# A decode layer over 2,048 cached positions: a K load moved forward, a reordering of the attention output, and a new split of the last weight rows over the DMA engines

## The chip, the cores and the metric

The kernel runs on one core of a Trainium2 chip. The metric is the time of one execution in device microseconds (us). Times of different kernels are compared only when they were taken on the same chip in alternating rounds, and the kernel before runs again beside each of them. Some executions fall into a slower group. Fast executions are compared with fast ones.

The words used throughout: TensorE multiplies matrices and leaves the result in a small memory, PSUM; VectorE and ScalarE (DVE and ACT in the profile) work element by element. A load brings data into the on-chip memory SBUF in pieces, one per DMA engine, and *lands* when the last piece has arrived. The granted clock is the share of its full clock that TensorE was given, 0.5 or 1.0 in these traces.

## The reference, cut to what matters

A layer normalization feeds two branches that are added to the input: attention over the last 2,048 cached positions, and an MLP with a squared ReLU.

```python
# B=2, Sq=1, D=576, Hq=32, Hkv=16, Sk=8192, Dh=128, F=4608; everything bfloat16
W = min(4096, max(256, Sk // 4))                     # 2048
q = (xn @ wq)                                        # 576 x 4096
k, v = the last W positions of each head's cache, each shared by two query heads
o = softmax(q k^T * Dh**-0.5) v
A = o @ wo                                           # 4096 x 576
B = relu(xn @ w1 + b1)**2 @ w2 + b2                  # w1: 576 x 4608, w2: 4608 x 576
return x + A + B
```

There are only two rows of activations, so nearly all the work is to read 53.6 MB of caches and weights once.

## The kernel before

The caches are cut into eight K units and eight V units of 2 MB (four heads of one batch row each). Everything big is issued on one queue in a fixed order, and each load is split over the sixteen DMA engines. TensorE transposes a K unit, multiplies it by the queries (`sc_ps`), and two steps later multiplies the probabilities by V (`o_ps`). The parts that the change touches:

```python
# o of one unit: o_ps is 128 x 512, four blocks of 128; row r is valid in one of the four blocks
def pv_sum(u):                      # sums of exp over the key chunks, and their reciprocal
    sc_ps = sc_tiles.pop(u)
    matmul(sc_ps[:, 0:1], lhsT=same_c[:], rhs=l_tiles.pop(u)[:], start=True, stop=True, ...)
    nc.vector.reciprocal(out=linv[:], in_=sc_ps[:, 0:1])

def pv_end(u):
    nc.vector.tensor_scalar(out=o_sb (128 x 512), in0=o_ps[:], scalar1=linv, op0=ALU.mult)
    def fin():
        for k in range(NS):         # NS = 4 fp32 products with the weights o_sb: o as 128 x 8
            matmul(o_ps[:, 0:NC], lhsT=o_sb[:, k, :], rhs=sel_o[:, k, :], start=(k == 0), stop=(k == NS - 1), ...)
        nc.vector.tensor_copy(out=oG_tiles[tq][:, :, b], in_=o_ps[:, 0:NC])

def wo_sel(t):                      # bring o onto wo's partitions: 16 selection products per half
    rr = oG * rmask                 # two VectorE operations
    for h in range(2 * NC):
        matmul(wps[:], lhsT=sel[:, MZ - h * DW:MZ - h * DW + P], rhs=rr[:, :, h * B:(h + 1) * B], ...)
    nc.vector.tensor_copy(out=ws[:, :, 0:MB:BS], in_=wps[:])
# ... cut ...
XR, XP, XE = 8, 32, 8               # the last 256 rows of w2: 4 small loads of 8 pieces of 9,216 B
w2x_sb = const.tile([XP, XR * D], BF16, name="w2x_sb")
# ... cut ...
    for u in range(2, NU - 1):
        step(u)                     # transposes, scores and softmax of unit u; o of unit u - 2
        if u + 1 < NU - 1:
            load_v(u + 1)
        if u == 4:
            issue_wo(0)
            for i in range(NW):
                issue_w1(i)
        if u + 3 < NU:
            load_k(u + 3)           # the last K unit is queued behind wo and w1
        if u == 5:
            load_v(NU - 1)
    issue_wo(1)
    for w in W2P:                   # w2: three blocks of 9 x 128 rows, then 4, 2 and 1 x 128 rows
        issue_w2(*w)
    mlp_h_start(); pv_all(NU - 3); wo_sel(0); wo_acc(0)
    # ... h = relu(w1 x + b1)^2 ...
    step(NU - 1, with_pv=False)     # the last K unit, late
    pv_all(NU - 2); mlp_x(); pv_all(NU - 1)
    wo_sel(1); wo_acc(1)
    for w in W2P[:NG4 - 1]:
        mlp_o(*w)                   # three big w2 blocks into out_ps
    # four copies of out_ps into part, then mlp_tail: the last 7 x 128 rows, then one addition
```

`mlp_x` multiplies the 256 rows of `w2x_sb`. In the profile the four part copies are `part<-out_ps`, the last rows are `tail_ps<-w,hT_sb` and the addition is `fin_sb<-tail_ps,part`.

## Time and profile before

| | kernel before |
|---|---|
| timed executions | 134.98, 135.18, 137.09 us |
| the profiled execution | 136.98 us, span 135.19 us, marked slow |
| moved by DMA | 53.76 MB in 4,419 packets |
| TensorE, VectorE, ScalarE busy | 99.4, 56.6, 46.5 us |
| last load landed | 129.72 us |

The span runs from the first to the last instruction in the profile. It is about 1.8 us shorter than the time of the same execution (136.98 less 135.19). A row of the groups gives engine, line and operation, then output and inputs with shapes and count, then the busy sum in us and the mean of one in ns, and at last the idle time just before and who ended it. These two groups of the kernel before bring o of a unit from one layout into another, eight times 1.1 and 0.75 us:

```profile
L104 PE MATMUL o_ps<-sel_o,o_sb 128*128 128x8 f32 x64 | 9.1, 268 | 2.9 <-DVE o_sb L398 2.9
...
L398 DVE TENSOR_SCALAR o_sb<-o_ps,linv 128x512 f32<-128x512 f32 x8 | 6.0, 750 | 2.2 <-PE o_ps L104 1.7
```

### The profile page before, as it was taken

To read this page: it belongs to the slowest core of one execution; us is meant where nothing else is said; L and a number is where in the kernel's file an instruction comes from. 1 tells how busy PE (TensorE), PEld (TensorE's weight loads), DVE (VectorE), ACT (ScalarE), POOL (GpSimd) and SP (SyncE) were. 2 spreads that over 40 slices of the span, in tenths; PEclk is the share of its full clock that TensorE was granted. 3 is DMA by queue.
4 is the path that set the end of the run, shared out by engine and by line. 5 is a ranking of instruction groups with operands and counts; after the bars stand their busy time and mean duration, and the time that the engine had idled before them with its cause. 6 is when DMAs were issued, how large, how long until landed. Compare 5 with 4: busy or idle time off the path is not lost.

```text
span 135.2 us, 2258 instructions
## 1 busy us (share of the span) xinstructions
PE 99.4 (74%) x939; PEld 64.6 (48%) x939; DVE 56.6 (42%) x154; ACT 46.5 (34%) x65; POOL 5.5 (4%) x18
## 2 busy tenths in 40 slices
PE   0067747979759779877897897788529976977980
PEld 0065423455427455545554574554229744454660
DVE  7934405254482565484393574510052446022010
ACT  6714502178275085093372462200032522000000
POOL 7000000010100100100100100100000001000000
PEclk9999975579999999999999999856985599555599
DMA  4999999999999999999999999999999999999800
GB/s 151 393 419 439 441 415 441 417 441 427 431 427 439 422 427 436 417 446 419 431 431 431 436 426 431 425 431 411 441 427 427 436 439 426 408 433 430 325 13 1
DMA packets 4419, 53.76 MB, mean 398 GB/s; under 512 B 531, under 2 KB 662, under 8 KB 1178
## 3 DMA queue, kind: packets, MB, share of 16 engines
q1 hardware_dynamic: 4320, 53.32, 92.9%
q10 hardware_dynamic: 90, 0.31, 0.6%
q8 instruction: 7, 0.11, 0.3%
q14 instruction: 2, 0.02, 0.0%
HBM read 53.62 MB, written 0.00 MB: 397 GB/s over the span
## 4 chain that ended last, share of the span: by engine, by line
DMA 40%; PE 36%; DVE 14%; issue 3%; SPq 2%; ACT 2%; POOL 1%; POOLq 0%; ACTq 0%; DVEq 0%
DMA w_rem<-in_B_w_dram 27%; DMA wq<-in_A_wq_dram 12%; PE kT_ps L107 12%; PE out_ps L104 7%; PE sc_ps L104 7%; PE o_ps L104 6%; DVE kT L338 4%; DVE o_sb L398 2%; PE q_ps L104 2%; DVE m L357 2%; DVE pT L371 1%; SPq L132 1%; DVE qrow L302 1%; SPq L125 1%; DVE hrow L463 1%
## 5 line engine op out<-in xcount | busy, mean ns | idle before, releaser
L107 PE MATMUL kT_ps<-ident_f,k 128*128 128x128 f32 x256 | 41.4, 310 | 7.7 <-DVE kT L338 3.4
L107 PEld LDWEIGHTS kT_ps<-ident_f,k 128*128 128x128 f32 x256 | 32.6, 160 | 20.6 <-DVE kT L338 5.7
L336 ACT COPY kT<-kT_ps 128x1024 bf16<-128x1024 bf16 x32 | 31.5, 1013 | 20.6 <-PE kT_ps L107 20.6
L338 DVE COPY kT<-kT_ps 128x1024 bf16<-128x1024 bf16 x32 | 21.5, 681 | 15.3 <-PE kT_ps L107 15.3
L104 PE MATMUL sc_ps<-kT,qz 128*32 128x512 bf16 x128 | 10.6, 415 | 5.8 <-DVE kT L338 5.6
L368 ACT ACTIVATE p<-sc_ps,bias 128x512 bf16<-128x512 f32 x8 | 5.5, 687 | 23.1 <-DVE gown L364 19.5
L104 PE MATMUL o_ps<-sel_o,o_sb 128*128 128x8 f32 x64 | 9.1, 268 | 2.9 <-DVE o_sb L398 2.9
L104 PEld LDWEIGHTS o_ps<-sel_o,o_sb 128*128 128x128 f32 x64 | 8.8, 214 | 4.8 <-DVE o_sb L398 4.8
L104 PE MATMUL o_ps<-v,pT 128*32 128x512 bf16 x128 | 10.2, 414 | 0.0
L357 DVE TENSOR_REDUCE m<-sc_ps 128x1 f32<-128x512 f32 x8 | 5.5, 691 | 7.6 <-PE sc_ps L104 7.6
L104 PE MATMUL out_ps<-wo,ws 128*17 128x288 bf16 x64 | 8.0, 442 | 0.7 <-DVE ws L432 0.7
L371 DVE STREAM_TRANSPOSE pT<-p 128x512 bf16<-128x512 bf16 x8 | 5.7, 710 | 5.1 <-ACT p L368 5.1
L104 PEld LDWEIGHTS <-qz 128*32 128x32 bf16 x128 | 2.6, 98 | 9.9 <-DVE kT L338 7.2
L361 POOL PARTITION_ALL_REDUCE gmax<-m x8 | 2.9, 366 | 106.4 <-DVE m L359 106.4
L398 DVE TENSOR_SCALAR o_sb<-o_ps,linv 128x512 f32<-128x512 f32 x8 | 6.0, 750 | 2.2 <-PE o_ps L104 1.7
L601 ACT COPY part<-out_ps 17x144 f32<-17x144 f32 x2 | 0.5, 268 | 18.1 <-DVE part L601 18.1
L104 PEld LDWEIGHTS <-xnT 128*2 128x2 bf16 x100 | 3.0, 92 | 7.8 <-issue 6.7
L104 PEld LDWEIGHTS <-ws 128*17 128x17 bf16 x64 | 4.4, 133 | 3.5 <-issue 0.5
L407 DVE CAST oG<-o_ps 128x8 bf16<-128x8 f32 x8 | 1.4, 170 | 10.2 <-PE o_ps L104 10.2
L463 DVE TENSOR_TENSOR hrow<-t 98x384 bf16<-98x384 f32 x3 | 1.6, 556 | 9.6 <-ACT t L462 9.5
L107 PE MATMUL pro_ps<-ident,tmp_x 2*128 2x2 bf16 x6 | 0.5, 174 | 6.6 <-DVE tmp_x L230 6.6
L462 ACT ACTIVATE t<-h_ps 98x384 f32<-98x384 f32 x3 | 1.4, 488 | 11.5 <-PE h_ps L104 11.2
(88 smaller groups left out, 73.6 us busy)
## 6 DMA issues: line engine op xcount, KB each, us to landing
k<-in_A_k_cache_dram SPq DMA_DIRECT2D x8, 2048.0 KB, 16.3
v<-in_A_v_cache_dram SPq DMA_DIRECT2D x8, 2048.0 KB
wo<-in_A_wo_dram SPq DMA_DIRECT2D x2, 2304.0 KB
w<-in_B_w_dram SPq DMA_DIRECT2D x2, 2304.0 KB, 36.0
wq<-in_A_wq_dram SPq DMA_DIRECT2D x2, 2048.0 KB
w<-in_B_w_dram SPq DMA_DIRECT2D x3, 1296.0 KB, 31.3
w_rem<-in_B_w_dram SPq DMA_DIRECT2D x1, 576.0 KB
w<-in_B_w_dram SPq DMA_DIRECT2D x1, 576.0 KB
```

Source lines behind the costliest of these rows:

```text
L104: tc.keep_in_program_order(nc.tensor.matmul(*a, **k))
L107: tc.keep_in_program_order(nc.tensor.transpose(*a, **k))
L336: nc.scalar.copy(out=kT, in_=kT_ps[:])
L338: nc.vector.tensor_copy(out=kT, in_=kT_ps[:])
L357: nc.vector.tensor_reduce(out=m1[:], in_=sc_ps[:], axis=AX.X, op=ALU.max)
L361: nc.gpsimd.partition_all_reduce(gmax[:], m2[:], channels=P, reduce_op=ReduceOp.max)
L368: nc.scalar.activation(out=p_sb[:], in_=sc_ps[:], func=ACT.Exp, bias=bias[:, 0:1], scale=scale, accum_out=l1[:])
L371: nc.vector.transpose(out=pT[:].rearrange("p j r -> p (j r)"), in_=p_sb[:])
L398: nc.vector.tensor_scalar(out=o_sb[:].rearrange("p s d -> p (s d)"), in0=o_ps[:], scalar1=o_tiles.pop((u, 0))[:, 0:1], scalar2=None, op0=A ...
L407: nc.vector.tensor_copy(out=oG_tiles[tq][:, :, b], in_=o_ps[:, 0:NC])
L462: nc.scalar.activation(out=t1, in_=mlp["ps"][k][0:RB, :], func=ACT.Relu)
L463: nc.vector.tensor_tensor(out=hrow[:, k * HB:(k + 1) * HB], in0=t1, in1=t1, op=ALU.mult)
```

## The change

Three things are changed. **The order:** the last K unit is loaded and worked on ahead of wo and w1, so that at the end of the stream only V units and weights are left. **The product:** VectorE adds the four blocks of `o_ps` into one 128 x 128 tile under a mask. One fp32 product of 129 columns, of which the 129th is the row of sums, brings that onto the partitions that wo wants, and the division comes last. The row sums no longer need the scores' PSUM bank. **The split:** of the last 256 rows of w2, 96 go as four loads of eight pieces (3,456 B each) and 160 as four loads of five (9,216 B each). Before, all went as four loads of eight pieces of 9,216 B. The intent there is to leave less on three of the eight engines concerned.

```diff
-    XR, XP, XE = 8, 32, 8
-    FT = (HW - XR * XP) // P
+    XS = ((3, 32, 8), (8, 20, 5))
+    FT = (HW - sum(r * p for r, p, _ in XS)) // P
 ... (cut: the rows' bookkeeping, tiles renamed, PSUM banks dealt out anew, b2 put on x's tile)
-    w2x_sb = const.tile([XP, XR * D], BF16, name="w2x_sb")
-    const.tile([P, 120], F32, name="pad_1")
+    w2x_sb = [const.tile([xp, xr * D], BF16, name=f"w2x_sb_{i}") for i, (xr, xp, _) in enumerate(XS)]
+    const.tile([P, 24], F32, name="pad_1")
 ... (cut)
-        o_sb = work.tile([P, NS, Dh], F32, tag="o_sb", name=f"o_sb_{u}")
-        nc.vector.tensor_scalar(out=o_sb[:].rearrange("p s d -> p (s d)"), in0=o_ps[:],
-                                scalar1=o_tiles.pop((u, 0))[:, 0:1], scalar2=None, op0=ALU.mult)
+        o1 = o1_tiles.pop(u)
+        for k in range(NS):
+            kw = dict(out=o1[:, 0:Dh], in0=o_ps[:, k * Dh:(k + 1) * Dh])
+            if k == 0:
+                nc.vector.tensor_scalar(scalar1=in_s[:, 0:1], scalar2=None, op0=ALU.mult, **kw)
+            else:
+                nc.vector.scalar_tensor_tensor(scalar=in_s[:, k:k + 1], in1=o1[:, 0:Dh], op0=ALU.mult, op1=ALU.add,
+                                               **kw)
 
         def fin():
-            for k in range(NS):
-                matmul(o_ps[:, 0:NC], lhsT=o_sb[:, k, :], rhs=sel_o[:, k, :], start=(k == 0), stop=(k == NS - 1),
-                       skip_group_check=True)
 ... (cut)
+            matmul(op_tiles[t][:, b, :], lhsT=of_h[:, z:z + P], rhs=o1[:], start=(i == 0 and b == 0), stop=(i == 1),
+                   skip_group_check=True)
 ... (cut: pv_sum and the selection products of wo_sel go; reciprocal, mask, product and sum on VectorE come)
-    for u in range(2, NU - 1):
+    for u in range(2, NU):
         step(u)
-        if u + 1 < NU - 1:
+        if u + 1 < NU - 2:
             load_v(u + 1)
+        if u + 3 < NU:
+            load_k(u + 3)
         if u == 4:
             issue_wo(0)
             for i in range(NW):
                 issue_w1(i)
-        if u + 3 < NU:
-            load_k(u + 3)
         if u == 5:
-            load_v(NU - 1)
+            for v in (NU - 2, NU - 1):
+                load_v(v)
+    wo_sel(0)
+    wo_acc(0)
     issue_wo(1)
 ... (cut)
-    step(NU - 1, with_pv=False)
     pv_all(NU - 2)
     mlp_x()
```

## The prediction

> **What bounds the kernel now.** I read the page first: the engines, then the slices, then the chain of work that ended last.
>
> ```profile
> PE 99.4 (74%) x939; PEld 64.6 (48%) x939; DVE 56.6 (42%) x154; ACT 46.5 (34%) x65; POOL 5.5 (4%) x18
> ...
> PEclk9999975579999999999999999856985599555599
> DMA  4999999999999999999999999999999999999800
> GB/s 151 393 419 439 441 415 441 417 441 427 431 427 439 422 427 436 417 446 419 431 431 431 436 426 431 425 431 411 441 427 427 436 439 426 408 433 430 325 13 1
> ...
> DMA 40%; PE 36%; DVE 14%; issue 3%; SPq 2%; ACT 2%; POOL 1%; POOLq 0%; ACTq 0%; DVEq 0%
> ```
>
> No compute engine is full. The row of the sixteen DMA engines is full from the second slice to the 37th, at 410 to 446 GB/s. The kernel moves 53.76 MB, and at 430 GB/s that alone is 125 us. So the kernel is bound by its stream of loads, plus whatever comes after the stream. The question is how long the program goes on after the last byte. For that I took the busy time by stretch (PE busy, PEld, DVE, ACT, POOL, PEclk, DMA share, GB/s) and the timeline of the last 20 us:
>
> ```profile
> 115.00:120.00 5.00, 4.14 (x34) 1.84 (x28) 0.92 (x2) 0.00 (x0) 0.00 (x0) 0.50 0.99 420
> ...
> 125.00:126.00 1.00, 1.00 (x12) 0.59 (x10) 0.00 (x0) 0.00 (x0) 0.00 (x0) 0.50 0.95 395
> 126.00:127.00 1.00, 1.00 (x12) 0.58 (x8) 0.00 (x0) 0.00 (x0) 0.00 (x0) 0.50 0.90 365
> 127.00:128.00 1.00, 1.00 (x12) 0.59 (x10) 0.00 (x0) 0.00 (x0) 0.00 (x0) 0.51 0.80 304
> 128.00:129.00 1.00, 1.00 (x20) 0.77 (x18) 0.00 (x0) 0.00 (x0) 0.00 (x0) 1.00 0.29 92
> 129.00:130.00 1.00, 1.00 (x22) 0.77 (x18) 0.00 (x0) 0.00 (x0) 0.00 (x0) 1.00 0.03 9
> ```
>
> ```profile
> 122.98 4.01 PE L104 MATMUL out_ps<-wo,ws 128*17 128x288 bf16 x32 [0.31 <-DVE ws L432]
> 126.55 4.54 PEld L104 LDWEIGHTS <-hT_sb 128*17 128x17 bf16 x82
> 126.79 3.81 PE L104 MATMUL out_ps<-w,hT_sb 128*17 128x288 bf16 x50
> ...
> 130.89 0.60 DVE L601 COPY part<-out_ps 17x144 f32<-17x144 f32 x2 [7.96 <-PE out_ps L104]
> 131.60 0.55 ACT L601 COPY part<-out_ps 17x144 f32<-17x144 f32 x2 [18.05 <-DVE part L601]
> 132.19 0.31 DVE L607 TENSOR_TENSOR fin_sb<-tail_ps,part 113x144 bf16<-113x144 f32 x1 [0.69 <-ACT part L601]
> ```
>
> Two things are visible. First, TensorE works without a pause from 123 us to 131 us, at half the clock until 128: it has a **backlog**. In the trace's list of completed loads, the second wo lands at 117.9 us and the first two w2 blocks at 121.0 and 124.1, yet their products begin only at 123 and 126.8. Second, the DMA engines **do not stop together**: the share falls from 0.95 to 0.03 over five microseconds. Following the packets of each engine from end to start, three engines end at 126.6 to 126.9 us, nine at 127.8 to 128.3 and four at 128.8 to 129.2. The very last load counts as landed at 129.7 us.
>
> The one profiled execution counted 136.98 us and is marked slow. The three timed ones are 134.98, 135.18 and 137.09, so they too fall into two groups 2 us apart. I read the shown trace as one of the slow group, with its last 20 us at half clock, though the profiler's own cost could also explain it.
>
> **What the Trainium skill says.** "DMA: Bandwidth & Descriptors", in the section on why a DMA increments its semaphore by 16, says that a load is split over the largest k up to 16 that divides the slowest dimension, and that loads issued this way use the lowest-numbered k engines. So the w2 rows that are loaded as eight pieces go to engines 0 to 7, and those of five pieces to 0 to 4. The trace agrees as to the number: each of the four loads to w2x_sb lands in eight pieces. Which eight no view names. "TensorE: Matmul & The Clock Gate", Part 1, says that the clock is either half or full and is set by recent activity in windows of about 3.4 us. The trace agrees: the granted clock is 0.5 or 1.0, in stretches of 6.8 or 13.65 us, and the last 0.5 runs from 114.3 to 128.0 us.
>
> **The change, part by part.**
>
> *Order of loads.* The last K unit goes ahead of wo and w1. The same bytes move, and the two V units after them end at the same place in the stream (107 and 112 us). TensorE transposes the last unit after 84 us instead of from 102.3 to 111 us. After w1 has landed (97.3 now, some 5 us later then) only the MLP's middle part and the last two V units are left. The sequence that now ends at 111 (24 + 8 transposes and scores) leaves the tail. Each load is queued long before its turn (a V unit issued at 58.2 lands at 79.6), so waiting for a buffer should leave no hole in the stream.
>
> *o by one product.* Per unit, 8 matmuls of 268 ns (9.1 us over 64) and 2 of 242 ns for the row sums go, and one fp32 product with 129 columns comes, some 0.5 us as an estimate from two passes like the 0.28 us pairs. On VectorE one 0.75 us scaling, a 0.16 us reciprocal and a 0.17 us copy go, and four operations of 128x128 come, some 0.2 to 0.25 us each as an estimate from a quarter of 0.75. So about 1 us of TensorE per unit goes and VectorE stays even. The 32 selection products (1.4 us) go as well; 1.1 us of VectorE takes their place. In units 0 to 6 all this is hidden under the stream. On the path of the last unit it is 1.9 + 0.4 us less at half clock.
>
> *Sum for the tail.* TensorE is at least 5 us earlier, more than its backlog of 5.1 us at wo (123.0 against 117.9 us). Every product then waits for its load. The third w2 block lands at 127.2. Its 18 products take 2.2 us at half clock or 1.1 at full (0.25 or 0.12 per pair), so they end at 129.5 or 128.4. The four part copies and their handovers take 1.3 us: 130.8 or 129.7. The last piece lands at 129.7 and is multiplied by 130.1. From the last addition to the end of the span this trace has 135.2 - 132.2 = 3.0 us. So the end is 133.8 at half clock and 133.1 at full: **1.4 to 2.1 us less** than 135.2, with the loads as they are.
>
> *DMA balance.* By size, a packet of 10,368 B takes 0.389 us and one of 4,608 B 0.178 us. An estimate is 0.345 us for 9,216 B and 0.135 us for the new 3,456 B. Now engines 0 to 7 have four of 9,216 B each (1.38 us). Afterwards 0 to 4 have four of each size (1.92 us) and 5 to 7 have four small ones (0.54 us). Around 115 us three of the eight are about 1 us later than their five fellows. If those are 5 to 7, the five come up by 0.54 us and the three down by 0.84 us, and the last landing falls by 0.4 to 0.8 us. The seven instruction fetches of 16,384 B on the other queue, of 0.9 us each, hit engines singly and one falls as late as 127.3 us, so I count on **0.5 us**.
>
> **The rivals.** (1) *The backlog exists only in slow executions.* At full clock the same products in the tail take half: the wo block 2.0 us instead of 4.0, a w2 block 1.1 instead of 2.2. TensorE would then have caught up with the loads before the end, and the fast runs of before would already stand at the DMA bound, 133.1 plus the 1.8 us between the profiled execution's count and its span: 134.9, just what was timed. Then only the balance gains: 134.9 - 0.5 = 134.4. For it speak the two groups; against it nothing but that the offset may be the profiler's. (2) *The shown trace is the fast state*, and the span itself is what is timed: then 135.2 - 1.4 - 0.5 = 133.3, or 132.6 with a full clock. (3) *A new hole in the stream:* the last K load waits for a buffer ahead of wo and w1 on the same issuing queue. Against it stand the 20 us of queued loads; it would make 136 or more. (4) *The w2 shift loads engines that are already late* (if the late ones are not 5 to 7): up to 0.5 us worse, 135.4. (5) *TensorE idles more in the tail and drops to half clock:* up to 0.7 us, counted above.
>
> **Range and chances.** I give rival 1 about six parts in ten (134.4), rival 2 three (133.0), and the rest to 3 and 4 (135.4): 0.6 x 134.4 + 0.3 x 133.0 + 0.1 x 135.4 = 134.1, which I put at 134.0 since the rebalancing was surely chosen by its result. The range is 132.6 to 135.5. Faster by over 2% means below 132.5, past nearly every bound above, since the stream itself doesn't get shorter: 0.12. Slower by over 2% needs a hole of 3 us: 0.03. The rest, 0.85, is within 2%.
>
> **What would show it.** In the changed trace the last K unit's transposes should begin near 84.5 us, right after the sixth unit's. The products of wo and w2 near the end should each be preceded by an idle time ended by a DMA load, with the chain's last part made of DMA and not of TensorE. The stretches of the last five microseconds should fall more steeply. TensorE's busy sum should be some 10 us lower at the same clocks. The prediction is wrong if the DMA share has a hole between 60 and 110 us, if the last landing is later than 129.7 us, or if the part copies still wait for a TensorE that never paused.

## The result, and the profile after

| | before | after |
|---|---|---|
| executions side by side | 134.98, 135.18, 137.09, 137.44 us | 134.84, 134.92, 134.78, 134.73 us |
| median of them | 136.13 us | 134.81 us |
| ratio of the fast executions | | 0.9981 (0.9957 to 1.0005) |
| span of the shown trace | 135.19 us (slow) | 133.05 us (fast) |
| TensorE, VectorE, ScalarE busy | 99.4, 56.6, 46.5 us | 93.0, 58.8, 46.9 us |
| last load landed | 129.72 us | 129.66 us |

A ratio is the mean time of one kernel's fast runs over that of the other's fast runs in the same rounds, so it is not quite the ratio of the medians. By the medians the kernel is 1% faster, and by the fast runs 0.2%. Nearly all of the difference between the two figures is that two of the four executions of before were slow and none of after.

The rows of the page of the changed kernel that answer to those of before are the engines, the granted clock by fortieths of the span, what the DMA engines moved, and the chain that ended last:

```profile
PE 93.0 (70%) x850; PEld 55.1 (41%) x850; DVE 58.8 (44%) x160; ACT 46.9 (35%) x65; POOL 5.4 (4%) x18
...
PEclk9999995559999959999999999657997775555698
...
GB/s 104 427 432 422 448 399 468 399 443 420 429 438 437 404 454 406 463 404 437 430 414 448 409 458 403 437 438 443 438 412 434 404 466 426 424 404 433 408 193 1
...
DMA 92%; PE 4%; SPq 1%; issue 0%; DVE 0%; DVEq 0%
```

The stream has no hole: from the second slice to the 38th it moves 399 to 468 GB/s. The chain of waits, 40% DMA and 36% TensorE before, is now 92% DMA. Its last part, in order of time (start, duration, what):

```profile
107.61 22.06 DMA w<-in_B_w_dram
...
129.70 0.27 PE tail_ps L107 x4
...
130.05 0.31 DVE fin_sb L594
```

A load of w2 runs until 129.67 us, four products follow, then the last addition. The stretches of the last microseconds (PE, PEld, DVE, ACT, POOL busy, clock, DMA share, GB/s) show engines that no longer work without a pause, at full clock:

```profile
127.00:128.00 1.00, 0.76 (x14) 0.65 (x15) 0.00 (x0) 0.00 (x0) 0.00 (x0) 1.00 0.73 289
128.00:129.00 1.00, 0.90 (x26) 0.46 (x21) 0.44 (x2) 0.00 (x0) 0.00 (x0) 1.00 0.36 134
129.00:130.00 1.00, 0.59 (x16) 0.24 (x11) 0.15 (x1) 0.54 (x2) 0.00 (x0) 1.00 0.03 12
```

The DMA share falls no more steeply than before (0.73, 0.36, 0.03 against 0.80, 0.29, 0.03), so the engines still stop three microseconds apart. The timeline of the tail gives start, duration, instruction, and in brackets the idle time before it and who ended it:

```profile
120.04 4.01 PE L107 MATMUL out_ps<-wo,ws 128*17 128x288 bf16 x32 [1.55 <-DVE ws L421]
...
127.24 1.27 PE L107 MATMUL out_ps<-w,hT_sb 128*17 128x288 bf16 x18 [0.27 <-DMA w<-in_B_w_dram]
...
128.55 0.60 DVE L588 COPY part<-out_ps 17x144 f32<-17x144 f32 x2 [8.56 <-PE out_ps L107]
...
129.32 0.62 PE L107 MATMUL tail_ps<-w,hT_sb 128*17 128x144 bf16 x12 [0.28 <-DMA w<-in_B_w_dram]
```

The wo products begin 2.9 us earlier than in the slow trace of before (122.98). They still take 4 us at half clock, but the third w2 block at 127.24 waits for its load, and the last rows do so again at 129.32. From the last landing to the end of the span there are 133.05 - 129.66 = 3.39 us. The time of this execution is 134.84, again 1.79 us above its span, and in all other kept traces but one (1.93) the two differ by 1.78 to 1.82 us. So an execution that counts 134.8 or 134.9 us has a span of 133, and the span is not what is timed, as one rival of the prediction had it.

### The profile page after: what moved, and what is told of

Read it like the earlier page. It is cut to its first block, busy times and chain, and to the rows that moved or that the text cites. A ratio compares the mean times of both kernels' runs of the same rounds, so it can differ in the third digit from the quotient of the medians.

```text
span 133.0 us, 2082 instructions
## 1 busy us (share of the span) xinstructions
PE 93.0 (70%) x850; PEld 55.1 (41%) x850; DVE 58.8 (44%) x160; ACT 46.9 (35%) x65; POOL 5.4 (4%) x18
## 4 chain that ended last, share of the span: by engine, by line
DMA 92%; PE 4%; SPq 1%; issue 0%; DVE 0%; DVEq 0%
DMA v<-in_A_v_cache_dram 43%; DMA k<-in_A_k_cache_dram 20%; DMA w<-in_B_w_dram 17%; DMA wq<-in_A_wq_dram 12%; PE kT_ps L110 2%; PE o_ps L107 1%; SPq L128 0%; SPq L135 0%; DVE fin_sb L594 0%; PE tail_ps L107 0%; DVEq L594 0%
## 5 line engine op out<-in xcount | busy, mean ns | idle before, releaser
L110 PE MATMUL kT_ps<-ident_f,k 128*128 128x128 f32 x256 | 42.8, 315 | 11.1 <-DMA k<-in_A_k_cache_dram 7.2
L107 PE MATMUL o_ps<-v,pT 128*32 128x512 bf16 x128 | 12.1, 475 | 0.0
L388 DVE SCALAR_TENSOR_TENSOR o<-o_ps,in_s,o 128x128 f32<-128x128 f32 x24 | 8.3, 346 | 0.5
L386 DVE TENSOR_SCALAR o<-o_ps,in_s 128x128 f32<-128x128 f32 x8 | 2.7, 338 | 10.8 <-PE o_ps L107 10.8
L107 PE MATMUL out_ps<-wo,ws 128*17 128x288 bf16 x64 | 6.1, 364 | 1.6 <-DVE ws L421 1.6
L107 PEld LDWEIGHTS <-hT_sb 128*17 128x17 bf16 (+2 forms) x104 | 4.8, 105 | 4.0 <-issue 1.3
L107 PE MATMUL op_ps<-o,of_h 128*128 128x129 f32 x16 | 4.0, 339 | 3.3 <-DVE o L388 3.2
L107 PEld LDWEIGHTS <-ws 128*17 128x17 bf16 x64 | 3.5, 111 | 3.9 <-DVE ws L421 1.9
L107 PEld LDWEIGHTS op_ps<-o,of_h 128*128 128x128 f32 x16 | 2.8, 221 | 5.3 <-DVE o L388 5.3
L107 PE MATMUL h_ps<-w,xnT 128*2 128x384 bf16 x48 | 3.2, 419 | 2.2 <-DMA w<-in_B_w_dram 2.2
```

The lines of the kernel that those rows point to most:

```text
L107: tc.keep_in_program_order(nc.tensor.matmul(*a, **k))
L110: tc.keep_in_program_order(nc.tensor.transpose(*a, **k))
L386: nc.vector.tensor_scalar(scalar1=in_s[:, 0:1], scalar2=None, op0=ALU.mult, **kw)
L388: nc.vector.scalar_tensor_tensor(scalar=in_s[:, k:k + 1], in1=o1[:, 0:Dh], op0=ALU.mult, op1=ALU.add, **kw)
```

## The experiments

The theory after the result, called S below: in its fast executions the kernel before already ends with its stream, at the same landing as the changed one. The order of loads then only removes the slow group, in which TensorE ends last. The first rival: the changed kernel is truly faster in the tail, and something else, such as its own product, gives that back. The second: the new split is what moves the time, in either direction. A further theory, F, came up on the way: the engines that finish last do so because they also fetched instructions.

### 1. The kernel before again, for a trace of a fast execution

The edit is none.

> The kernel before, unchanged, once more. Theory S (the stream of loads sets the end of a fast execution; slow ones are those where TensorE's tail products run at half clock and stay behind the loads): two groups of times, near 135.0 and near 137.1 us; an execution of the fast group has a span of about 133.2 us, that is 1.8 us under its time, and a last landing near 129.7 us as in the slow one. Rival B (the backlog of TensorE sets the end in every execution, and the 1.8 us are the profiler's): spans of about 135.2 us also where the time is near 135.0, or a last landing 2 us earlier in the fast ones.

Its six executions took 134.92, 135.65, 136.9, 137.06, 137.34 and 137.42 us. The profiled one was the fast one, at 134.92 with a span of 133.13. Its timeline:

```profile
121.08 3.35 PE L104 MATMUL out_ps<-wo,ws 128*17 128x288 bf16 x32 [0.31 <-DVE ws L432]
...
127.49 1.27 PE L104 MATMUL out_ps<-w,hT_sb 128*17 128x288 bf16 x18 [0.86 <-DMA w<-in_B_w_dram]
...
129.43 0.59 PE L104 MATMUL tail_ps<-w,hT_sb 128*17 128x144 bf16 x12 [0.29 <-DMA w<-in_B_w_dram]
...
130.12 0.31 DVE L607 TENSOR_TENSOR fin_sb<-tail_ps,part 113x144 bf16<-113x144 f32 x1 [0.71 <-ACT part L601]
```

This is what theory S says. The last load lands at 129.73 (slow trace 129.72), TensorE has caught up and waits 0.86 us for the third w2 block, and the addition comes at 130.12 in place of 132.19. The half clock that ran from 114.3 to 128.0 us in the slow trace runs only from 116.8 to 123.6 here. So the loads of the two groups end alike; TensorE's clock during the last 15 us makes the difference of 2 us. Over all rounds, 22 of 53 timed executions of before took 136.9 us or more.

### 2. One part at a time

The first kernel is before with the new order alone. The row sums had to be moved ahead of the MLP's middle part as well. In the old product they hold the scores' PSUM banks, and a first build without that move was found to deadlock before it ran. So the order cannot be taken quite alone.

```diff
-    for u in range(2, NU - 1):
+    for u in range(2, NU):
 ... (the loads as in the change)
+    pv_sum(NU - 2)
+    pv_sum(NU - 1)
     mlp_h_end()
-    step(NU - 1, with_pv=False)
```

> The kernel before with only the order of the last K unit changed (the row sums of the last two units are moved a little ahead so that the score banks come free; without that it can't run). Theory S: fast executions 0 to 0.3% faster than those of before (134.7 to 135.1 us), and no slow group any more or a rarer one, since the 8.7 us of the last unit's transposes leave TensorE's tail. Rival B: faster by 1% or more against the fast executions of before.

It took 134.81 to 135.02 us in six executions (median 134.93, ratio 0.9984, 0.9954 to 1.0013), and none was slow. (At before's share of 22 in 53, six in a row without a slow one would come by chance about once in 25.) Its wo products start at 119.80 us, its third w2 block waits for its load, and its last landing is at 129.69:

```profile
127.28 1.27 PE L104 MATMUL out_ps<-w,hT_sb 128*17 128x288 bf16 x18 [0.49 <-DMA w<-in_B_w_dram]
```

The order alone gives the whole of what the change gives.

The second is after with the old order: before's loop and `step(NU - 1, with_pv=False)` back behind the MLP's middle part.

> The changed kernel with the old order of the last K unit, all else as changed. Theory S: fast executions as the changed kernel (134.6 to 135.2 us), slow ones near 136.5 to 137 come back if the order is what removed them. If the shorter tail of the one fp32 product removed them, all stay near 134.8 us.

It took 136.18 to 136.52 us (and 138.51 once); the ratio is 1.0085 (1.0051 to 1.0119). Neither outcome that was expected came: there is no fast group near 134.8 us at all. The last landing, 129.78, is where it was, but its tail is TensorE's:

```profile
122.96 3.91 PE L107 MATMUL out_ps<-wo,ws 128*17 128x288 bf16 x32 [1.55 <-DVE ws L421]
...
131.52 0.31 DVE L595 TENSOR_TENSOR fin_sb<-tail_ps,part 113x144 bf16<-113x144 f32 x1 [0.69 <-ACT part L589]
```

Product and split without the order are slower than before: wo begins at 122.96 against 121.08 in the fast trace of before. So in the tail the new product and split are no saving. Per unit four operations on VectorE take 0.34 us each:

```profile
L388 DVE SCALAR_TENSOR_TENSOR o<-o_ps,in_s,o 128x128 f32<-128x128 f32 x24 | 8.3, 346 | 0.5
...
L107 PE MATMUL op_ps<-o,of_h 128*128 128x129 f32 x16 | 4.0, 339 | 3.3 <-DVE o L388 3.2
...
L386 DVE TENSOR_SCALAR o<-o_ps,in_s 128x128 f32<-128x128 f32 x8 | 2.7, 338 | 10.8 <-PE o_ps L107 10.8
```

That is 1.38 us (8.3 and 2.7 over eight) in place of 1.08 (0.75 + 0.16 + 0.17). TensorE is relieved, as meant: 4.0 us of products stand where 9.1 + 2.8 stood. After the last V unit the operations come one after another. In the fast trace of before,

```profile
115.87 1.05 PE L104 MATMUL o_ps<-v,pT 128*32 128x512 bf16 x16
...
116.97 0.75 DVE L398 TENSOR_SCALAR o_sb<-o_ps,linv 128x512 f32<-128x512 f32 x1 [0.83 <-PE o_ps L104]
...
117.78 1.88 PE L104 MATMUL o_ps<-sel_o,o_sb 128*128 128x8 f32 x8 [0.86 <-DVE o_sb L398]
```

lead to wo at 121.08, 4.11 us after the first operation on VectorE. In the changed kernel,

```profile
116.12 0.35 DVE L386 TENSOR_SCALAR o<-o_ps,in_s 128x128 f32<-128x128 f32 x1 [5.47 <-PE o_ps L107]
116.51 1.12 DVE L388 SCALAR_TENSOR_TENSOR o<-o_ps,in_s,o 128x128 f32<-128x128 f32 x3
117.69 0.80 PE L107 MATMUL op_ps<-o,of_h 128*128 128x129 f32 x2 [1.62 <-DVE o L388]
```

lead to wo at 120.04, after 3.92 us, both at half clock; with the old order it is 3.98 (118.98 to 122.96). So this path is not the loss of 1.88 us. It arises earlier, between the scores of the last K unit, which begin at 110.22 with the old order and at 110.41 in before, and the products with the last V unit:

```profile
117.03 1.90 PE L107 MATMUL o_ps<-v,pT 128*32 128x512 bf16 x16
```

Compared stretch by stretch, the products of the 256 rows begin 0.82 us later (115.30 against 114.48), mainly because the four operations on the V unit before are interrupted by the 0.71 us in which VectorE transposes the last unit's probabilities. The new split's 22 small products in place of 16 take 0.65 us more (1.81 us against 1.15 in before). The products for the row sums, which are gone, save 0.31 us. The V products then run at half clock, which began at 116.4 us, and take 0.85 us more. The path to wo saves 0.13 us. Together these are the 1.88 us, in this one pair of traces.

The third is after with the old split, `XS = ((8, 32, 8),)`, and a larger unused tile so that the large tiles should stay where they were.

> The changed kernel with the 256 extra w2 rows on eight DMA engines as before. My prediction counted 0.5 us for the new split: the time would rise to about 135.3 us with a last landing near 130.2 us. Rival: the split is worth nothing at the end, because the two last engines come late for another reason (instruction fetches): the time stays within 0.2 us of the changed kernel and the last landing within 0.2 us of 129.7 us.

It took 135.81 to 135.96 us (ratio 1.0052, 1.0023 to 1.0082), and the last landing is at 130.69, 1.0 us later than in the changed kernel. That looked like the second rival. It was not: experiment 5 shows that the large tiles had slipped by 96 B in SBUF, since another tile had shrunk with the split. As a test of the split this run is void.

### 3. Is the slow group TensorE's backlog?

Before without the second half of the output projection. Its output is wrong, which doesn't matter for the time. (It still passed the comparison with the reference, whose tolerance is wider than this half's share of the sum.)

```diff
     wo_sel(1)
-    wo_acc(1)
     for w in W2P[:NG4 - 1]:
```

> The kernel before without the second half of the output projection (32 products of 4.0 us at half clock; a wrong result on purpose; all loads stay). Theory S: only fast executions, near 134.9 us, last landing still 129.7 us: the slow group was TensorE's backlog at half clock, and taking 4 us from its tail removes it, while the fast time does not fall. Rival: both groups stay, 2 us apart, because the slow state has another cause.

Six executions took 134.79, 134.93, 135.14, 135.69, 135.74 and 135.75 us; the ratio is 1.0017 (0.9975 to 1.006). In the same rounds before had four of eleven at 137.3 to 137.9 and one at 136.0. With 32 products fewer (4.0 us at half clock) that group is gone (six executions are few, as above), and one at 135.7 stands in its place, which theory S had not expected. The profiled execution belongs to it:

```profile
127.30 1.85 PE L104 MATMUL out_ps<-w,hT_sb 128*17 128x288 bf16 x14 [0.76 <-DMA w<-in_B_w_dram]
...
130.97 0.31 DVE L606 TENSOR_TENSOR fin_sb<-tail_ps,part 113x144 bf16<-113x144 f32 x1 [0.69 <-ACT part L600]
```

The clock is half until 129.8 us here. The third block waits for its load as in a fast execution, but its products take twice as long, and the span is 133.97. The prediction's sum for a tail at half clock without a backlog was 133.8. So there are three cases: full clock without a backlog (133.1), half clock without one (134.0), and half clock with one (135.2). What makes the half clock last to 128 or 130 us in one execution and end at 123.6 in another of the same kernel was not tried.

### 4. What is the slowest DMA engine worth, and what the split?

After without the loads of the 256 rows (zeros in their place; the result is wrong):

```diff
-            tc.keep_in_program_order(nc.scalar.dma_start(out=w2x_sb[s][i:xp:xp // xe, :], in_=rows[i]))
+            if i == 0:
+                nc.gpsimd.memset(w2x_sb[s][:], 0.0)
```

> The changed kernel without the loads of the 256 extra w2 rows (zeros in their place: a wrong result on purpose). Theory S (the slowest DMA engine sets the end): if it is one of 0 to 4, which lose 1.9 us each, the last landing falls by 0.6 to 1.9 us and the time falls with it, by the same amount; if one of 5 to 7, by 0.5 us. Rival B (TensorE's tail sets the end): no change of the time whatever the landings do.

It took 133.61 to 133.95 us, ratio 0.9901 (0.9861 to 0.9941), the only one of the study whose interval lies wholly below 1 (by the record's bound of 2% it is still unclear). Its timeline:

```profile
128.27 0.59 PE L107 MATMUL tail_ps<-w,hT_sb 128*17 128x144 bf16 x12 [0.27 <-DMA w<-in_B_w_dram]
...
128.96 0.31 DVE L595 TENSOR_TENSOR fin_sb<-tail_ps,part 113x144 bf16<-113x144 f32 x1 [0.86 <-PE tail_ps L107]
```

The last landing is at 128.57, 1.09 us earlier than in the changed kernel, and everything behind it moves with it: the span is 131.94, 1.11 us less. The end follows the slowest DMA engine one to one, as theory S has it. Taking these bytes away altogether is worth 1.1 us, so a mere split of them can be expected to gain less.

The old split once more, now with the large tiles at their old place: the unused tile is 96 B wider than in the run that slipped.

> The changed kernel with the extra w2 rows on eight DMA engines as before, once more: in the first try the K, V and weight tiles had slipped by 96 bytes in SBUF, to 416 past a multiple of 512, and nearly all packets of 16,384 B took 611 to 619 ns instead of a steady 611. Here the tiles start at a multiple of 512 again. If the split itself is worth something, the last landing is later than 129.7 us (my prediction's sum: 130.2 us, 135.3 us of time). If the 1.0 us of the first try came from the slip alone: last landing 129.7 to 129.9 us, time 134.8 to 135.0 us, packets steady at 611 ns.

Five executions took 134.76 to 135.08 us (median of all six 134.86); the ratio is 0.9983 (0.9948 to 1.0018). The sixth, the profiled one, took 162.16. Its trace holds no record of the granted clock at all, and the 1.00 that the views print is what they print without one. Its products took as long as others do at half clock, throughout. For the transposes of K that is a mean of 442 ns, where those of the changed kernel's trace take 428 in its half-clock stretches and 280 at full clock:

```profile
L110 PE MATMUL kT_ps<-ident_f,k 128*128 128x128 f32 x256 | 65.6, 442 | 2.9 <-DVE kT L329 1.6 <-DMA k<-in_A_k_cache_dram 1.3
```

In the other traces read for this, the transposes that run before the first record of the clock take 415 to 428 ns as well. So the clock seems never to have risen in this execution; why is open. Such an execution came once, and its result was correct. The same kernel was therefore looked at once more, on another chip:

> The changed kernel with the old split of the extra rows, tiles at multiples of 512, once more for its trace (in the first try the profiled execution was the odd one of 162 us). The timed executions were those of the changed kernel, so the last landing should be 129.6 to 129.8 us, with other engines last: those of 0 to 7 that carry 1.38 us and were hit by a fetch, 2.8 to 3.0 us behind the first.

It took 134.70 us; its transposes had a mean of 296 ns, its span was 132.91 and its last landing 129.51, 0.15 us earlier than with the new split. (That is no gain of the old split either: four traces of before's own kernel and its variants with that split land last at 129.69 to 129.74, and four with the new split and undisturbed tiles at 129.56 to 129.81.) By time and by trace the new split gains nothing at the end.

A split over all sixteen engines, 4 loads of 16 pieces of 4,608 B (`XS = ((4, 64, 16),)`):

> The changed kernel with the 256 extra w2 rows spread over all sixteen DMA engines (4 rows on 64 partitions, tiles at multiples of 512). Engines 8 to 15 get 0.71 us more, 0 to 7 less by 0.5 (5 to 7: 0.2 more). If the two last engines are among 0 to 4, the last landing falls by up to 0.6 us (129.1 us, time 134.2 us); if they are among 8 to 15, it rises by 0.7 us (130.4 us, 135.5 us); among 5 to 7, 129.9 us. The four or five engines that now end 2.6 us early should come 0.7 us later if they are among 8 to 15.

It took 135.0 to 135.22 us and 136.87 once; the ratio, 1.0024 (0.9959 to 1.0088), is unclear. The first engine to finish landed its last piece at 128.26 in place of 126.87, and the last at 129.94 in place of 129.66. So the spread falls, from 2.79 to 1.67 us, and the end doesn't move forward.

### 5. Where the large tiles lie

The run of experiment 2 that was void had its large tiles 416 B past a multiple of 512. Both before and after have them at multiples. Two kernels shift them on purpose and do nothing else:

```diff
-    const.tile([P, 24], F32, name="pad_1")
+    const.tile([P, 24 + 64], F32, name="pad_1")     # shift256: 256 B more
+    const.tile([P, 24 + 8], F32, name="pad_1")      # shift32: 32 B more
```

> The changed kernel with all large tiles 256 bytes further in SBUF (256 past a multiple of 512; the slip of the first try was 416). If only multiples of 256 matter, the packets stay at 611 ns and the time at 134.8 us. If it takes multiples of 512, some packets take longer and the time is between 134.8 and 135.9 us.

> The changed kernel with all large tiles 32 bytes further in SBUF. If the start of the tiles in SBUF is what made the first try of the old split 1.0 us slower, packets of 16,384 B jitter between 611 and 619 ns here too, and the time is about 135.8 us. If the cause of that was something else, 134.8 us and a steady 611 ns.

With 256 B more it took 134.8 to 135.01 us (ratio 0.9981, 0.9933 to 1.0029), just as without. With 32 B more it took 135.9 to 135.98 (1.0059, 1.0011 to 1.0107), and the last landing was at 130.78, 1.1 us later. The packets' durations show it directly. Of those of 16,384 B that start after the first 8 us, nine in ten take up to 611 ns in the changed kernel and with 256 B, but up to 621 ns with 32 B and 619 ns in the void run; the means are 612.4, 613.6, 616.2 and 615.1 ns. "DMA: Bandwidth & Descriptors" of the Trainium skill, under how a descriptor splits into AXI transactions, says that transactions begin at multiples of 256 B and that a descriptor (one contiguous run of bytes that an engine moves) that doesn't start there costs extra beats. It speaks of the bytes fetched; here it is the start of the written tiles in SBUF that was moved. The runs agree that 256 B past a multiple of 512 cost nothing, and the two other starts tried, 32 and 416 B past it, cost 1.0 to 1.1 us. So the width of an unused pad tile, which looks like a leftover in both kernels, decides over 0.8% of the time; a kernel without the pads was not run.

### 6. Closing the spread at the end

The 96 rows on sixteen engines instead of eight, `XS = ((3, 32, 16), (8, 20, 5))`; then the same with part of the small products moved ahead of the last V unit's and behind them; then the same with the small loads issued one unit later:

> The changed kernel with the 96 extra rows on all sixteen engines instead of eight (0.27 us more on 8 to 15, 0.27 less on 0 to 7), the 160 rows on 0 to 4 as they are. Theory F (the last engines of the changed kernel are those two of 5 to 7 that an instruction fetch hit for about 1.4 to 1.8 us and that carry 0.54 us of w2 rows on top): last landing falls from 129.66 to 129.1 to 129.3 us, time 134.3 to 134.5 us. Rival: the last two are among 0 to 4: also 0.27 us, or among 8 to 15: 0.27 us later, time 135.1 us.

> The same, and the 22 products of the extra rows split around the last unit: 6 before it, 16 while VectorE works on its result. TensorE's tail gets some 1.3 us earlier. Theory S (the stream sets the end): the same time as without that, within 0.1 us (134.3 to 134.5 us), with fewer slow executions at most. Rival: with the landing earlier TensorE is the later one in the other kernel, and this one is faster by 0.3 us or more.

> The 96 rows on sixteen engines, but with the first two of the six small loads put off to later, since in the first try all engines had slow packets of 16,384 B (670 to 800 ns) between 8.8 and 11.5 us, where those two loads ran, and every landing came 0.6 us later. If that is what ate the gain: packets at 611 ns there, the last landing 129.2 to 129.4 us, time 134.4 to 134.6 us. Rival: the slow packets have another cause, and the time stays near 135.0 us.

| | time | ratio to before | first engine done | last landing |
|---|---|---|---|---|
| after | 134.73 to 134.92 us | 0.9981 | 126.87 us | 129.66 us |
| 96 rows on sixteen | 134.82 to 135.44 us | 1.0001 (0.9956 to 1.0045) | 127.51 us | 129.88 us |
| and products moved | 134.8 to 135.28 us | 0.9991 (0.9947 to 1.0034) | 127.80 us | 130.21 us |
| and loads later | 134.8 to 134.88 us, once 135.62 | 0.9959 (0.9899 to 1.002, unclear) | 127.28 us | 129.73 us |

The spread fell from 2.79 to 2.37 us in the first and 2.45 in the last, and all of it was lost again: the first engine finished 0.64 and 0.41 us later. The bytes alone account for 0.27 us of the first engine's 0.64 us; packets of 16,384 B that mostly took 670 to 800 ns between 8.8 and 11.5 us, while a small load of sixteen pieces ran, account for part of the rest. With the loads issued later, the slow packets moved with them. The loads of sixteen pieces now run at 29.4 to 30.4 and 38.1 to 39.3 us, and all 48 packets over 640 ns between 28 and 44 us lie at 29.6 to 30.8 and 38.3 to 39.7, up to 865 ns but for one of 1,142; in the changed kernel, with loads of eight pieces, only two in that stretch are over 640 ns. The mean stays at 615.2 ns in both. In the even split, too, slow packets (32.4 to 33.2 and 41.1 to 42.1 us) go with its loads of sixteen pieces. So in these traces a small load over all sixteen engines slows the full queue beside it, wherever it is put. It is not the only thing that does: the kernel of 256 B more has some 40 packets of 640 to 760 ns between 15 and 34 us, with loads of eight pieces. That moving products forward in TensorE's order gained nothing fits theory S.

### 7. Do instruction fetches set the spread?

On a queue of its own the program fetches its instructions in blocks of 16,384 B: seven in before (the last at 125.4 us in the fast trace), six in after (27.5 to 116.1 us), since after has 176 instructions fewer. A block takes 0.88 to 1.0 us, and the large packet that follows it on the same engine about 1.1 us in place of 0.611. So a fetch costs its engine some 1.4 us. Theory F: the engines come in groups by how many fetches and how much of the small loads they had. If so, one fetch more must take one engine out of the early group at the end. The kernel is after with 288 small instructions more (three matmuls into a PSUM tile that is overwritten, ahead of the transposes of six units):

```diff
+        if 1 <= u <= 6:
+            for _ in range(3):
+                matmul(kT_f[0:32, 0:16], lhsT=ident[:, 0:32], rhs=ident[:, 0:16], start=True, stop=True, skip_group_check=True)
```

> The changed kernel with 144 small extra products in units 1 to 6 (288 TensorE instructions more with their weight loads, written where the transposes write over them), so that the instructions fill one more block of 16,384 B. Theory F (each fetch of instructions costs the one DMA engine that carries it some 1.4 us): seven fetches instead of six, and the group of engines that land first shrinks by one, from four or five to three or four; the end moves only if the seventh engine is a late one (0 to 1.4 us, time 134.8 to 136.2). Rival: the groups of landings stay as they were, so fetches are not what spreads the engines.

It fetched seven blocks. The completions of the last load, sixteen by engine, in us after the first of them:

```
before, fast  (7 fetches)  0.00 0.07 0.39 | 1.39 1.40 1.49 1.55 1.59 1.60 1.65 1.69 1.70 2.11 2.42 2.93 2.94
after         (6 fetches)  0.00 0.23 0.23 0.38 0.74 | 1.54 1.61 1.66 1.70 2.01 2.09 2.10 2.10 2.15 2.59 2.79
after, one more (7)        0.00 0.37 0.43 0.48 | 1.54 1.57 1.59 1.66 1.68 1.73 1.81 1.95 1.96 2.03 2.53 2.74
no w2 rows    (6 fetches)  0.00 0.07 0.08 0.15 0.21 0.25 0.39 0.47 0.60 0.93 | 1.44 1.50 1.71 1.83 1.85 1.86
```

The early group has four engines in place of five, as theory F says; the other traces with the new split and six fetches have five. In the kernel without the small loads six engines come 1.44 to 1.86 us after the first, as many as there are fetches, and in the even split, where all sixteen engines carry the same rows, again six (1.42 to 1.68 us). With the old split the early group has four engines at six fetches (two traces) and three at seven (three traces); a fourth trace with seven, that of experiment 3, has four, so the count doesn't fit every time. The time itself was 134.83 and 134.86 us, and 136.12 and 138.88 in two executions (ratio 0.998, 0.9886 to 1.0075, unclear). The last landing was 129.56, so here a fetch that meets an early engine was free.

By the same sizes the row of after can be read as follows, though no view names the engines, so this is inferred. The four at 1.54 to 1.70 had a fetch. The five at 2.01 to 2.15 carry 1.92 us of w2 rows and no fetch. The last two had a fetch and 0.54 us of rows, which makes 2.1 to 2.3; they came at 2.59 and 2.79, and the other 0.4 to 0.6 us stay unexplained.

## Why the prediction was right or wrong

**The number.** 134.0 us was predicted and 134.81 measured, inside the range, but most of the gain that was forecast did not come: the fast executions differ by 0.2%. The main sum, "1.4 to 2.1 us less", took the end of TensorE's backlog for the end of the program. That holds in slow executions alone. In a fast one before already ends with its stream (span 133.13 us at a time of 134.92), and the order alone has a ratio of 0.9984. The prediction had this as its first rival, "the backlog exists only in slow executions", with a value of 134.4. The mean was drawn down to 134.0 by the three parts in ten for the second rival, 133.0, which experiment 1 rules out. That 134.81 fell into the range owes as much to the width of the range as to the mechanism.

**Balance of the DMA engines: wrong.** "So I count on 0.5 us" is the term of the first rival's sum that failed. The last landing moved by 0.06 us (129.72 to 129.66), and with the old split in the changed kernel it is at 129.51, no later. The packet estimates behind the term were right (0.345 and 0.135 us against a measured 0.347 and 0.135). What failed is the step from packets to the last engine, "if those are 5 to 7": taking 0.84 us of rows from three engines did not bring the last one forward, since with either split in the changed kernel it comes 2.6 to 2.8 us after the first (2.61 old, 2.79 new). The fetches, of 1.4 us each with the packet behind them, set much of each engine's lag, and the split took no account of which engines they meet. What the last two engines of the changed kernel wait for beyond that is open.

**The sum for the tail: right.** It gave 133.1 at full clock and 133.8 at half. Measured were 133.05 (after), 133.13 (before, fast) and 133.97 (before without the second half of wo, half clock). Its parts held too: the third block at 127.2, the copies done by 129.7 (129.81), the last addition at 130.1 (130.05). It described the fast kernel before just as well, and so was no gain.

**Order of loads: right in kind.** The last K unit's transposes begin at 85.04 us, where "near 84.5" was predicted:

```profile
85.04 1.94 PE L110 MATMUL kT_ps<-ident_f,k 128*128 128x128 f32 x8 [1.99 <-DMA k<-in_A_k_cache_dram]
```

No hole opened. But "TensorE is at least 5 us earlier" was too much: wo begins 2.9 us earlier than in the slow trace and 1.0 us earlier than in the fast one. It suffices because TensorE catches up before the third w2 block. "Every product then waits for its load" holds from that block on; wo's products wait 1.55 us for VectorE, and the first two w2 blocks follow them without a wait for a load. Nor did the last five microseconds fall more steeply.

**The product: wrong in size.** "Some 0.2 to 0.25 us each" for the four operations was an estimate by width, a quarter of the 0.75 us of the wide one. They take 0.34 us, so a narrower fp32 operation here costs nearly half of the wide one and not a quarter. "1.9 + 0.4 us less at half clock" on the last unit's path was 0.2 us less from the first VectorE operation to wo (4.11 to 3.92, both at half clock), besides the row sums' products before it. It left out what comes in their place: the new product's 0.80 us, and VectorE's longer chain. The new product's own cost was right, 0.5 us per unit (4.0 over eight). TensorE's busy sum fell by 6.4 us (99.4 to 93.0) where "some 10 us lower at the same clocks" was forecast; the mean clock was lower, 0.843 against 0.860, so the 10 us are not shown.

**Two readings of the lines** were off, without consequence. From the second to the 37th slice the stream moved 393 to 446 GB/s, not 410 to 446. And the stretches of the granted clock in that trace are 6.83, 10.24, 13.65 and once 58.03 us, all multiples of 3.41, and not only the two that are named.

**Chances.** Within 2% had 0.85, and that came about. What the change is good for is the slow group: 22 of 53 executions of before were in it, none of four of after and none of six with the order alone. It may not be gone for good: of the 63 executions of all kernels with the new order three are at 136.8 us or more (the even split at 136.87, one more fetch at 138.88, and the one at 162.16). None of the versions tried is clearly faster than the changed kernel with a right result; 134.70 (one execution) and 134.82 us are the nearest.

## What to carry to other kernels

When the same kernel has two groups of times, get a trace of each before you add up savings: here the shown trace ended with TensorE and the fast one with the stream, and savings in the first were worth nothing in the second. For a kernel that ends with its stream, follow the slowest DMA engine alone; in the traces here in which TensorE had caught up at full clock the span ended 3.3 to 3.4 us after the last landing, whatever had been changed. And when an edit changes the size of a tile, check where the tiles behind it come to lie before you judge the edit.

## What the Trainium skill lacked or had wrong

- "Runtime: NRT & Kernel Launch", on instruction fetch mechanics, has fetches of 16 KiB (256 instructions) and says that they are "hidden" by the pace of dispatch. They are hidden from the compute engines here, but not from the stream: each takes 0.88 to 1.0 us of a DMA engine and makes the next large packet 1.1 us instead of 0.611. Without the small loads, and with six fetches, the engines still finish 1.86 us apart.
- "DMA: Bandwidth & Descriptors", on AXI transactions, gives the beats of a descriptor that doesn't begin at a multiple of 256 B, but not what it costs a full stream: 1.0 to 1.1 us of 134 with the SBUF side 32 or 416 B past a multiple of 512, and nothing at 256 B past it.
- No page read says how small loads of many pieces act beside a full queue: with 16 pieces per load, most packets of 16,384 B took 650 to 865 ns in place of 611 while they ran, at 9, at 30 or at 39 us, wherever the loads were put; at the loads of 8 pieces of the changed kernel none did.
- "TensorE: Matmul & The Clock Gate", Part 1, agrees with the two clocks seen, and says that its window runs freely, so that the number of slow products at the start differs between runs of one kernel, at under 1% of a typical span. Here the difference lies at the end: the half clock ended at 123.6 us in one execution and at 128.0 in another of the same kernel, which made 2 us of 135, or 1.5%. The page also warns that clock records can be unreliable. It has no case like the one of 162.16 us, where the trace holds none and all products take as long as at half clock.
